# A retention layer and a gated feed-forward on one core: the same steps in another order, with other buffer slots

## Chip, cores and metric

One core of a Trainium2 chip runs the whole program in one launch. The metric is device time in microseconds (us) of that core; three runs of the kernel before are at hand, and one profiled execution with its trace. Engines are named as in the profile: PE (TensorE; PEld is its weight load), DVE (VectorE), ACT (ScalarE), POOL (GpSimd), SP (the queue that issues the DMAs).

## What is computed

For 4 batches, 8 heads, 768 positions and head size 64 a retention (linear attention with decay) is computed, and on its output a feed-forward with a convolution of three taps as gate:

```python
for t in range(S):
    state = gamma[None, :, None, None] * state + np.einsum('bhd,bhe->bhde', k[:, :, t], v[:, :, t])
    y[:, :, t] = scale * np.einsum('bhd,bhde->bhe', q[:, :, t], state)
...
h = np.maximum(x @ w_in, 0.0)                 # 512 -> 1024
...
for k in range(K):
    conv_out += conv_w[k][None, None, :] * hp[:, k:k + S, :]
gate = 1.0 / (1.0 + np.exp(-conv_out))
return (h * gate @ w_out).astype(np.float32)  # 1024 -> 512
```

## The kernel before, in words

All data are fp32. The retention is computed in chunks of 64 positions: 24 chunks `n` (two pairs of batches, 12 chunks each), all eight heads of both batches of a pair at once. Two chunks make a unit `u` of 128 positions (12 units), and on units the feed-forward works. There is no loop in the program that sets the order: every step has a name, and the string `ORDER` lists all 1352 of them; the program emits each step's instructions as it comes by in that list. Each engine then runs its own instructions strictly in that order and waits by semaphores for what others make.

The steps of a chunk `n` on PE are multiplications 64x64 in fp32: `scores/n` (k times q, into `ps_s`), `mix/n` (the masked scores times v into `ps_y`, together with the scores of the next chunk) and `across/n` (q times the state so far into the same `ps_y`, together with the new chunk's part of the state, into `ps_st`). A `mix` or an `across` has 32 such multiplications in two streams (16 at the first and last chunks of a pair), and each multiplication stands in the trace as two matmuls with two weight loads. Between them `masked/n` (DVE) multiplies the scores by the mask, `scale_v/n` scales v (on ACT or DVE), `carry/n` (ACT) copies the state from `ps_st` for the next chunk, and `decay/n` (DVE) reads `ps_y` and writes x.

Matrix products of the feed-forward are made in fp32r from split operands: a value is its rounded head and the rest, and three products (head x head, head x rest, rest x head) are summed. `x_head`, `x_rest` split x; the steps `w_...` split the weights, piece by piece as `load_w/i` brings them (0 to 7 of w_in, 8 to 15 of w_out, 16 the taps). `mm1/u/f` (12 matmuls 128x256 into `ps_m`) makes one block of 128 of the 1024 hidden features of a unit; `relu/u/p` (ACT) takes two such blocks to a buffer `h`; `seam` (POOL) copies or clears the border columns of `h` between units; `conv_tap` (ACT) and `conv_side` (DVE) compute the three taps; `gate` (ACT), `gated` (DVE), `g_head` (ACT) and `g_rest` (DVE) make the split factor `g`; `mm2/u/t/p/h` (6 matmuls 128x512, 256 columns at the very end) multiplies it by w_out into `ps_o`; `put` (ACT) and `store` (SP) bring it out. For units 8 to 11 the first product is made of seven smaller ones (`prod/v/j/q`, 12 matmuls each, a scheme with sums of operands: `sum_w`, `diff`, `head`, `sum_p`, `copy_p`), in place of `mm1`.

Buffers have numbered slots: `BUFS` says how many of a kind, and `SLOTS` gives, in order of use, which slot each new buffer takes (31 of `h`, 7 of `x`, 4 of `g`, 3 of `cv`, 2 of `ps_o`, `ps_y`, `ps_m`, `m` each). A step that writes a slot waits until the readers of its former content are done. `HELD` makes seven loads wait for a given step. Neither `BUFS` nor `HELD` differs in the new version.

Of the kernel before, what the change touches and what calls it, by code (L numbers as in the profile page):

```python
# [80 lines left out]
    w_shift/1 w_abs/2 mix/0 w_sign/1 w_clamp/2 w_shift/2 carry/0 load_kv/2 scores/1 w_power/1 load/3 w_head/1 load_w/3  # L81
    masked/1 load_w/16 scale_v/1 w_low/1 w_sign/2 mix/1 decay/0 across/1 make_gy/0 carry/1 w_head/2 w_rest/1 load_kv/3
    scores/2 load/4 decay/1 scale_v/2 masked/2 x_head/0 w_add/1 scores/3 x_head/1 w_power/2 w_abs/3 x_rest/0 mix/2
    x_rest/1 load_w/4 w_clamp/3 across/2 scale_v/3 w_shift/3 masked/3 mm1/0/0 load/5 w_low/2 load_w/5 w_rest/2 mm1/0/1
    w_sign/3 decay/2 w_head/3 w_add/2 carry/2 mix/3 w_abs/16 w_power/3 w_abs/4 w_rest/3 across/3 x_head/2 masked/4
    relu/0/0 w_low/3 mm1/0/2 load/6 scale_v/4 w_add/3 x_rest/2 mm1/0/3 carry/3 decay/3 w_clamp/4 x_head/3 w_shift/4
    mix/4 w_abs/5 x_rest/3 relu/0/1 w_clamp/5 across/4 make_gy/1 load_w/6 load_w/7 mm1/1/0 w_shift/5 w_sign/4 w_sign/5
    w_head/4 mm1/1/1 w_power/4 carry/4 w_power/5 w_head/5 masked/5 mm1/1/2 scale_v/5 w_rest/4 w_clamp/16 w_low/4
    relu/1/0 mm1/1/3 w_shift/16 load/7 scale_v/6 w_sign/16 w_add/4 w_power/16 w_low/5 mix/5 relu/1/1 decay/4 w_abs/6
    w_rest/5 across/5 w_clamp/6 w_low/16 w_add/5 mm1/1/4 carry/5 load/8 decay/5 load_w/8 x_head/4 masked/6 w_abs/7  # L90
    mm1/0/4 w_shift/6 w_add/16 w_sign/6 w_power/6 w_head/6 mix/6 make_gy/2 conv_tap/0/2 across/6 w_clamp/7 scale_v/7
    w_shift/7 masked/7 mm1/0/5 load/9 load_w/9 w_sign/7 carry/6 conv_tap/0/3 w_low/6 mm1/1/5 relu/0/2 w_rest/6
    w_head/7 seam/0/2/0 w_power/7 seam/0/1/0 w_add/6 mix/7 w_rest/7 w_abs/8 across/7 w_low/7 x_head/5 relu/1/2 w_add/7
    mm1/0/6 load/10 x_rest/4 w_clamp/8 x_rest/5 mm1/0/7 w_shift/8 scale_v/9 w_sign/8 mm1/2/0 relu/0/3 masked/8 w_abs/9
# [5 lines left out]
    seam/0/2/2 w_sign/11 mix/10 carry/9 load/12 conv_side/0/3/0 relu/2/1 conv_side/0/1/0 across/10 x_rest/6 scale_v/11  # L100
    masked/11 mm1/2/5 load/13 w_power/11 w_low/11 w_head/11 mm1/2/6 conv_side/0/2/2 carry/10 w_sign/10 relu/2/2
    w_power/10 w_head/10 mm1/3/0 conv_side/0/0/2 conv_tap/0/4 decay/10 scale_v/12 w_rest/11 mm1/3/1 decay/9 x_head/8
    conv_side/0/4/0 w_add/11 mm1/2/7 relu/3/0 w_low/10 load_w/14 x_head/9 w_rest/10 mix/11 relu/2/3 w_add/10 w_abs/12
    seam/2/3/0 across/11 load_w/15 seam/1/0/0 w_abs/13 masked/12 seam/1/1/0 w_clamp/12 seam/0/3/2 mix/12 x_rest/9
    load/14 seam/2/1/0 scale_v/13 seam/2/0/2 across/12 conv_side/0/1/2 w_shift/12 mm1/3/2 load/15 w_clamp/13
    w_shift/13 masked/13 mm1/3/3 w_sign/12 decay/12 x_rest/8 mm1/3/4 relu/3/1 w_sign/13 x_head/10 w_power/12 w_head/12
    mm1/3/5 w_low/12 gate/0/0 w_rest/12 conv_tap/0/5 carry/12 mm1/4/0 w_add/12 gated/0/0 w_abs/14 conv_side/0/5/0
    g_head/0/0 mm1/4/1 conv_side/0/4/2 relu/3/2 conv_side/0/3/2 decay/11 mix/13 g_rest/0/0 conv_side/0/5/2
    conv_tap/0/6 across/13 w_clamp/14 gate/0/1 w_power/13 masked/14 mm2/0/1/0/0 carry/13 load/16 scale_v/14
    conv_tap/0/7 x_rest/10 relu/4/0 mm1/3/6 x_head/11 gated/0/1 w_head/13 conv_side/0/6/0 w_rest/13 mm1/3/7  # L110
    conv_side/0/7/0 decay/13 mm2/0/0/0/0 w_low/13 conv_side/0/6/2 w_shift/14 mix/14 w_sign/14 g_head/0/1 relu/3/3
    g_rest/0/1 across/14 w_head/14 seam/3/3/0 conv_side/0/7/2 gate/0/2 seam/2/2/2 masked/15 mm2/0/0/1/0 load/17
    seam/1/1/2 conv_tap/1/0 gated/0/2 seam/3/1/0 carry/14 x_rest/11 gate/0/3 mm1/4/2 w_add/13 x_head/12 conv_tap/1/1
    scale_v/16 w_abs/15 mm1/4/3 w_power/14 x_head/13 conv_side/1/1/0 w_rest/14 g_head/0/2 w_clamp/15 mm2/0/1/1/0
    relu/4/1 w_low/14 seam/4/1/0 gated/0/3 seam/2/2/0 mm1/5/0 conv_side/1/0/0 seam/1/2/2 w_shift/15 seam/1/0/2
    g_rest/0/2 mm1/5/1 w_sign/15 conv_tap/1/4 scale_v/15 mm1/5/2 g_head/0/3 relu/5/0 g_rest/0/3 mm2/0/1/2/0
    conv_side/1/1/2 conv_tap/1/2 w_add/14 conv_tap/1/5 conv_side/1/0/2 mm1/5/3 decay/14 gate/1/0 x_rest/13 w_head/15
    mm1/4/4 conv_tap/1/3 conv_side/1/3/0 conv_side/1/2/0 mm2/0/0/2/0 w_power/15 conv_side/1/3/2 conv_side/1/2/2
    w_rest/15 mix/15 gated/1/0 across/15 g_head/1/0 masked/16 relu/5/1 conv_side/1/5/0 mix/16 load/18 g_rest/1/0
    seam/4/1/2 seam/1/3/2 w_low/15 conv_tap/1/6 mm1/5/4 seam/3/2/0 gate/1/1 seam/5/1/2 w_add/15 conv_side/1/5/2  # L120
    mm1/5/5 decay/15 conv_side/1/6/0 masked/17 mm1/4/5 gated/1/1 g_head/1/1 mm2/0/0/3/0 carry/15 g_rest/1/1
    conv_tap/1/7 relu/5/2 conv_side/1/7/0 across/16 conv_tap/2/0 conv_side/1/6/2 conv_side/1/4/0 scale_v/17
    conv_side/1/4/2 mm2/0/1/3/0 load/19 conv_side/1/7/2 gate/1/3 mm1/4/6 gate/1/2 put/0/1/0 gated/1/2 mm1/4/7
    g_head/1/2 put/0/0/0 g_rest/1/2 carry/16 gated/1/3 mm2/1/0/0/0 decay/16 g_head/1/3 conv_tap/2/2 g_rest/1/3 mix/17
    relu/4/3 conv_side/2/2/0 relu/4/2 conv_side/2/0/0 across/17 conv_tap/2/1 seam/4/2/2 x_head/14 seam/2/1/2
    mm2/1/0/1/0 load/20 conv_tap/2/4 seam/3/0/2 store/0/1/0 conv_tap/2/3 seam/4/3/0 conv_side/2/4/0 store/0/0/0
    seam/3/1/2 conv_tap/2/5 conv_side/2/1/0 seam/2/3/2 mm2/1/1/0/0 conv_side/2/2/2 seam/4/2/0 conv_side/2/3/0
    seam/4/0/2 conv_side/2/1/2 seam/5/0/0 conv_side/2/0/2 mm2/1/0/2/0 seam/3/3/2 conv_side/2/5/0 gate/2/0 seam/5/2/0
    masked/18 seam/3/0/0 x_head/15 conv_side/2/5/2 seam/4/0/0 mm1/5/6 carry/17 gated/2/0 seam/3/2/2 seam/5/1/0
    conv_side/2/4/2 g_head/2/0 seam/5/0/2 mm1/5/7 gate/2/2 g_rest/2/0 gated/2/2 mm2/1/0/3/0 conv_side/2/3/2 x_rest/15  # L130
    gate/2/1 gated/2/1 mm2/1/1/1/0 put/1/0/0 scale_v/18 relu/5/3 store/1/0/0 decay/17 seam/5/3/2 mm2/2/1/0/0
    g_head/2/1 conv_tap/2/6 conv_side/2/6/0 mix/18 scale_v/19 g_rest/2/1 across/18 masked/19 mm2/1/1/2/0 x_rest/14
    carry/18 load/21 conv_tap/3/0 decay/18 conv_tap/2/7 scale_v/20 x_head/16 mm2/1/1/3/0 conv_side/3/0/0 g_head/2/2
    conv_side/3/0/2 conv_tap/3/1 conv_side/2/7/0 mm1/7/0 conv_side/2/6/2 g_rest/2/2 x_rest/12 mm2/2/1/1/0
# [727 lines left out]
```

## Time and profile before

| | us |
|---|---|
| runs (three) | 335.62, 335.98, 338.96 |
| median | 335.98 |
| span of the profiled execution, first to last instruction | 335.6 |
| PE busy in it | 327.6 |
| DVE busy | 288.1 |
| ACT busy | 207.6 |

The span is one execution's time from its first to its last instruction; the runs' times are measured around whole executions without a profile. An engine's busy time counts overlapping instructions once. Matmuls are pipelined and their ends are modelled in the trace, so two matmuls that follow each other overlap.

### The profile page before, as it was taken

How to read it: one execution, taken by the hardware profiler on the slowest of the kernel's cores; microseconds unless marked ns; L12 is line 12 of the kernel's file. 1: busy time of each engine (PE TensorE's matmuls, PEld its weight loads, DVE VectorE, ACT ScalarE, POOL GpSimd, SP SyncE). 2: the span in 40 equal slices, each digit the busy share in tenths (PEclk: the TensorE clock that was granted, in tenths of full speed). 3: DMA queues.
4: the chain of work that ended last, by engine and by line, in shares of the span. 5: the costliest groups of instructions: out<-in, count | busy, mean ns of one | idle time of the engine just before them, and what ended most of it. 6: DMA issues, size and time to landing. Idle time of an engine off the chain costs nothing.

```text
span 335.6 us, 10804 instructions
## 1 busy us (share of the span) xinstructions
PE 327.6 (98%) x4666; PEld 293.4 (87%) x4666; DVE 288.1 (86%) x562; ACT 207.6 (62%) x430; POOL 24.2 (7%) x100
## 2 busy tenths in 40 slices
...
GB/s 248 350 366 323 229 296 281 273 273 241 182 127 128 2 128 127 191 93 158 100 33 26 166 2 34 32 0 34 31 2 31 34 0 64 2 63 0 64 63 63
DMA packets 10415, 40.77 MB, mean 121 GB/s; under 512 B 1280, under 2 KB 1792, under 8 KB 7808
## 3 DMA queue, kind: packets, MB, share of 16 engines
...
q8 instruction: 36, 0.59, 0.7%
...
## 4 chain that ended last, share of the span: by engine, by line
PE 96%; DVE 2%; issue 1%; ACT 0%; ACTq 0%; DVEq 0%
PE ps_o L783 40%; PE ps_m L570 27%; PE ps_s L390 6%; PE ps_m L690 5%; PE ps_y L690 5%; PE ps_st L390 5%; PE ps_y L390 4%; PE ps_o L312 3%; PE ps_s L690 2%; DVE rw L417 0%; DVE m L493 0%; DVE x L431 0%; DVE gy_sb L348 0%; DVE wi_lo L556 0%; DVE g L509 0%
## 5 line engine op out<-in xcount | busy, mean ns | idle before, releaser
L570 PE MATMUL ps_m<-xu,wi_hi 128*128 128x256 f32 x512 | 91.6, 281 | 0.0
L570 PEld LDWEIGHTS ps_m<-xu,wi_hi 128*128 128x128 f32 x512 | 78.9, 188 | 1.9
L570 PE MATMUL ps_m<-xu,wi_lo 128*128 128x256 f32 x256 | 71.5, 279 | 0.0
L783 PE MATMUL ps_o<-h,g 128*128 128x512 f32 (+1 forms) x200 | 63.4, 382 | 0.0
L390 PE MATMUL ps_y<-rw 64*64 64x64 f32 x1472 | 49.3, 220 | 1.7 <-issue 1.7
L570 PEld LDWEIGHTS ps_m<-xu,wi_lo 128*128 128x128 f32 x256 | 48.5, 189 | 0.0
L390 PEld LDWEIGHTS ps_y<-rw 64*64 64x64 f32 x1472 | 45.5, 135 | 2.4 <-issue 2.3
L754 ACT ACTIVATE cv<-cv 128x512 f32<-128x512 f32 x48 | 30.1, 629 | 21.9 <-DVE cv L748 21.9
L764 ACT CAST g<-cv 128x512 fp32r<-128x512 f32 x48 | 29.6, 618 | 21.9 <-DVE cv L759 17.3
L783 PEld LDWEIGHTS ps_o<-h,g 128*128 128x128 f32 x200 | 37.2, 188 | 6.7
L769 DVE TENSOR_TENSOR g<-cv,g 128x512 fp32r<-128x512 f32 x48 | 32.9, 689 | 10.5 <-ACT g L764 10.0
L748 DVE SCALAR_TENSOR_TENSOR cv<-h,cw_sb,cv 128x256 f32<-128x256 f32 x64 | 29.4, 479 | 1.4 <-ACT cv L743 1.2
L390 PEld LDWEIGHTS ps_s<-rw 64*64 64x64 f32 x768 | 24.7, 134 | 6.3 <-issue 3.4
L390 PE MATMUL ps_s<-rw 64*64 64x64 f32 x768 | 28.2, 221 | 1.3 <-DVE rw L417 1.0
L390 PE MATMUL ps_st<-rw 64*64 64x64 f32 x704 | 25.3, 219 | 0.9 <-ACT rw L358 0.6
L358 ACT ACTIVATE rw<-rw,consts_sb 128x128 f32<-128x128 f32 x64 | 20.4, 391 | 7.3 <-DMA rw<-in_qkv 7.3
L390 PEld LDWEIGHTS ps_st<-rw 64*64 64x64 f32 x704 | 22.8, 135 | 2.1 <-issue 0.8
L790 ACT COPY o_sb<-ps_o 128x512 f32<-128x512 f32 (+1 forms) x25 | 14.1, 565 | 12.1 <-PE ps_o L783 12.1
L417 DVE TENSOR_TENSOR rw<-ps_s,consts_sb 128x512 f32<-128x512 f32 x24 | 16.5, 686 | 4.4 <-PE ps_s L390 4.4
L743 ACT ACTIVATE cv<-h,cw_sb 128x256 f32<-128x256 f32 x32 | 16.0, 506 | 5.4 <-DVE g L769 5.4
L783 PE MATMUL ps_o<-h_g,g 128*128 128x512 f32 (+1 forms) x50 | 19.3, 388 | 0.0
L783 PE MATMUL ps_o<-h_m,g 128*128 128x512 f32 (+1 forms) x50 | 19.3, 388 | 0.0
...
## 6 DMA issues: line engine op xcount, KB each, us to landing
rw<-in_qkv SPq DMA_DIRECT2D x20, 1024.0 KB, 6.1
...
```

Of the source, the lines that this page charges most:

```text
L358: nc.scalar.activation(v[:, :, g], v[:, :, g], AF.Copy, scale=by[:, g : g + 1])
L390: nc.tensor.matmul(out, lhsT, rhs, start=start, stop=stop, skip_group_check=True)
L417: nc.vector.tensor_tensor(out=rw[n][:, 1], in0=s_ps.pop(n), in1=mask_sb.unsqueeze(1).broadcast_to([P, 2, NPAIR, C]), op=ALU.mult)
L570: nc.tensor.matmul(h_ps[u, p][:, odd], w[:, k, fs], x[:, k].rearrange("p b t -> p (b t)"), start=(i == 0), stop=(i == len(products) - 1),)
L690: nc.tensor.matmul(ps[:, i], w[k][:, fs], x[:, k].rearrange("p b t -> p (b t)"), start=(i == m == 0 and q in (1, 6, 5, 7)), stop=(m == len ...
L743: nc.scalar.activation(cvs[u, p][:, i], hs[u, p][:, i, :, 1 : P + 1], AF.Copy, scale=cw_sb[:, f, 1:2])
L748: nc.vector.scalar_tensor_tensor(out=cv, in0=h[:, :, k : k + P], scalar=cw_sb[:, f, k : k + 1], in1=cv, op0=ALU.mult, op1=ALU.add)
L754: nc.scalar.activation(cvs[u, p], cvs[u, p], AF.Sigmoid)
L764: nc.scalar.copy(gs[u, p][:, 0], cvs[u, p])
L769: nc.vector.tensor_tensor(out=lo, in0=cvs.pop((u, p)), in1=hi.bitcast(F32), op=ALU.subtract)
L783: nc.tensor.matmul(ps, g, w[f][:, cs], start=(f == 0 and i == 0), stop=(f == NF - 1 and i == 2))
L790: nc.scalar.copy(o[:, :n], o_ps.pop((u, t, h))[:, :n])
```

## The change

The list `ORDER` has the same 1352 steps. Its first 223 names are the same; from there on the steps stand in another succession, and the strings of `SLOTS` give the buffers other slots. On PE the two lists agree up to the end of `mix/9`, which lies between the first seven `mm1` steps of unit 1 and its last, `mm1/1/7`; behind it PE has `mm1/2/2` before and `across/9` now. A few functions are changed so that steps can stand in the new places: what was taken out of a dictionary at its last use now stays there, and a border column (`seam`) or a `relu` creates its buffer `h` if it is the first to touch it.

```diff
 SLOTS = {
-    "ps_o": "010101010101101001011001010",
-    "g": "0123012301230132001031203120312031203120312031203120312031203120",
+    "ps_o": "010110010101101001011010011",
+    "g": "0123012301230123012302130320130212302310231023120321032102302310",
...
-    "h": "0123456789abcdefghijklmnopqrstu0146235c9fdjilorpuc50639fjildoprujl9f",
-    "cv": "012102101201201201021020210212012012120012102012",
+    "h": "0123456789cabdfgijkelhomnqtprus0641253c9idflorj6up50c39dlifor5j6l0df",
+    "cv": "012102012201021020120120210121201021021002120102",
 }
 ORDER = """
...
-    w_low/8 w_sign/9 mix/8 decay/6 w_head/9 scale_v/10 across/8 masked/9 w_rest/8 mix/9 relu/2/0 load/11 w_power/9
...
+    across/8 masked/9 seam/1/2/0 sum_w/0/0 carry/8 w_rest/8 mix/9 across/9 load/11 seam/0/0/2 conv_side/0/0/2
...
     def masked(n):
-            out=rw[n][:, 1], in0=s_ps.pop(n), in1=mask_sb.unsqueeze(1).broadcast_to([P, 2, NPAIR, C]), op=ALU.mult
+            out=rw[n][:, 1], in0=s_ps[n], in1=mask_sb.unsqueeze(1).broadcast_to([P, 2, NPAIR, C]), op=ALU.mult
...
-        hs[u, p] = buf("h", [P, 2, 2, UH])
-        ps = h_ps.pop((u, p)).rearrange("p i (b t) -> p i b t", b=2)
-        nc.scalar.activation(hs[u, p][:, :, :, 1 : P + 1], ps, AF.Relu)
+        ps = h_ps[u, p].rearrange("p i (b t) -> p i b t", b=2)
+        nc.scalar.activation(inside(u, p), ps, AF.Relu)
...
-    def inside(u, p):
+    def h_of(u, p):
         if (u, p) not in hs:
             hs[u, p] = buf("h", [P, 2, 2, UH])
-        return hs[u, p][:, :, :, 1 : P + 1]
+        return hs[u, p]
+
+    def inside(u, p):
+        return h_of(u, p)[:, :, :, 1 : P + 1]
...
     def seam(u, p, side):
-        column = lambda v, i: hs[v, p][:, :, :, i : i + 1]
+        column = lambda v, i: h_of(v, p)[:, :, :, i : i + 1]
```

Place 1, PE at the end of `mix/9` (rows `ps_s` and `ps_y` with the chunks' buffers `rw`), before:

```order
L390 MATMUL ps_s_1218<-rw_1061 64x64 x2
L390 MATMUL ps_y_0_1217<-rw_946 64x64 x2
L570 MATMUL ps_m_0_1260<-xu_2_835,wi_hi_69 128x256 x2
L570 MATMUL ps_m_0_1260<-xu_2_835,wi_lo_70 128x256
L570 MATMUL ps_m_0_1260<-xu_2_835,wi_hi_69 128x256 x2
```

and now (`ps_st` is the state, which `across/9` adds to):

```order
L393 MATMUL ps_s_1223<-rw_1061 64x64 x2
L393 MATMUL ps_y_0_1222<-rw_946 64x64 x2
L393 MATMUL ps_st_193<-rw_946 64x64 x2
L393 MATMUL ps_y_0_1222<-rw_946 64x64 x2
L393 MATMUL ps_st_193<-rw_946 64x64 x2
```

`across/9` has moved up to `mix/9`, ahead of `mm1` steps of units 1 and 2.

Place 2, PE at the end of `across/17`, before:

```order
L390 MATMUL ps_st_1663<-rw_2011 64x64 x2
L390 MATMUL ps_y_0_2463<-rw_2011 64x64 x2
L783 MATMUL ps_o_0_2449<-h_g_1494,g_1_2348 128x512
L783 MATMUL ps_o_0_2449<-h_k_1593,g_1_2348 128x512
L783 MATMUL ps_o_0_2449<-h_g_1494,g_1_2348 128x512
```

and now:

```order
L393 MATMUL ps_st_1644<-rw_2300 64x64 x2
L393 MATMUL ps_y_0_2543<-rw_2300 64x64 x2
L393 MATMUL ps_s_2651<-rw_2648 64x64 x2
L393 MATMUL ps_y_1_2650<-rw_2330 64x64 x2
L393 MATMUL ps_s_2651<-rw_2648 64x64 x2
```

`mix/18` has moved up to `across/17`, where an `mm2` step stood; the same has been done with `mix/15` behind `across/14` and with `mix/21` behind `across/20`.

Place 3, SP's loads (`rw` of chunks 11 to 18, `g` of pieces 12 to 15 of w_out), before:

```order
L329 DMA rw_1253<-in_qkv 128x2048
L457 DMA g_0_1292<-in_w_out 128x1024
L457 DMA g_1_1335<-in_w_out 128x1024
L329 DMA rw_1413<-in_qkv 128x2048
L329 DMA rw_1469<-in_qkv 128x2048
L457 DMA g_3_1553<-in_w_out 128x1024
L457 DMA g_2_1614<-in_w_out 128x1024
L329 DMA rw_1658<-in_qkv 128x2048
L329 DMA rw_1695<-in_qkv 128x2048
L329 DMA rw_1875<-in_qkv 128x2048
L329 DMA rw_2011<-in_qkv 128x2048
```

and now:

```order
L332 DMA rw_1288<-in_qkv 128x2048
L460 DMA g_0_1507<-in_w_out 128x1024
L332 DMA rw_1576<-in_qkv 128x2048
L332 DMA rw_1630<-in_qkv 128x2048
L460 DMA g_3_1775<-in_w_out 128x1024
L332 DMA rw_1828<-in_qkv 128x2048
L332 DMA rw_1851<-in_qkv 128x2048
L460 DMA g_1_1926<-in_w_out 128x1024
L460 DMA g_2_1983<-in_w_out 128x1024
L332 DMA rw_2060<-in_qkv 128x2048
L332 DMA rw_2300<-in_qkv 128x2048
```

The last two pieces of w_out (`load_w/15`, `load_w/14`) have moved down behind `load/15`, directly ahead of `load/16`, and take slots of `g` that `mm2/0/0/0/0` and `mm2/0/1/1/0` read.

## Rows read from the trace of the kernel before

**Rows 1.** The page: span, then busy time, share and instructions of each engine.
```profile
span 335.6 us, 10804 instructions
...
PE 327.6 (98%) x4666; PEld 293.4 (87%) x4666; DVE 288.1 (86%) x562; ACT 207.6 (62%) x430; POOL 24.2 (7%) x100
```

**Rows 2.** Window: span, busy PE, PEld, DVE, ACT, POOL (count), PEclk, DMA share.
```profile
60.69:332.55 271.86, 270.54 (x3304) 244.03 (x3294) 235.91 (x462) 170.24 (x347) 22.04 (x86) 1.00 0.24 82
```

**Rows 3.** All waits of PE from 60 us on: total, times, longest.
```profile
PE ps_y L390 <- issue: 1.3, 1, 1.3
```

**Rows 4.** Timeline of PE around that wait: start, length, what.
```profile
80.42 0.28 PE L390 MATMUL ps_s<-rw 64*64 64x64 f32 x4
82.02 0.27 PE L390 MATMUL ps_y<-rw 64*64 64x64 f32 x2 [1.31 <-issue]
```

**Rows 5.** The page's DMA queues: packets, MB, share of 16 engines.
```profile
q8 instruction: 36, 0.59, 0.7%
```

**Rows 6.** Chain of work, in order of time: an earlier wait of PE.
```profile
27.09 0.30 issue
27.39 0.27 PE ps_s L390 x2
```

**Rows 7.** The same view, four stretches from 27.39 on.
```profile
27.39:60.56 33.17, 33.15 (x894) 32.04 (x897) 31.96 (x64) 21.72 (x50) 1.80 (x8) 1.00 0.79 275
27.39:69.67 42.28, 42.26 (x1149) 40.95 (x1152) 40.95 (x82) 26.94 (x60) 2.49 (x13) 1.00 0.77 270
27.39:78.08 50.69, 50.67 (x1277) 49.16 (x1280) 49.26 (x97) 32.44 (x74) 2.49 (x13) 1.00 0.78 270
27.39:82.02 54.63, 53.30 (x1403) 51.64 (x1403) 51.84 (x102) 35.33 (x79) 2.88 (x15) 1.00 0.78 268
```

**Rows 8.** DMA queue, five windows: 24.95:25.05, 79.7:79.8, 61:61.1, 73.05:73.15, 66.7:66.9.
```profile
q8 instruction: 1, 0.02, 55.2%
q8 instruction: 1, 0.02, 57.8%
q8 instruction: 1, 0.02, 75.3%
q8 instruction: 1, 0.02, 58.2%
q8 instruction: 1, 0.02, 38.9%
```

**Rows 9.** Chain of work: pieces in order of time (start, length, what).
```profile
58.81 0.20 PE ps_s L390 x2
...
61.85 5.85 PE ps_m L570 x48
67.70 0.20 PE ps_st L390 x2
...
98.23 1.36 PE ps_o L783 x6
99.59 0.20 PE ps_s L390 x2
101.61 1.59 PE ps_o L783 x6
103.20 2.83 PE ps_m L570 x24
```

**Rows 10.** Chain of work in windows 85:90 and 107.5:111.4: `mm1` alone.
```profile
84.99 5.10 PE ps_m L570 x45
107.43 4.01 PE ps_m L570 x34
```

**Rows 11.** The line of `masked`: duration in ns, shortest, median, longest.
```profile
L417 DVE TENSOR_TENSOR rw<-ps_s,consts_sb x24: 681/684/693, 10.6 to 195.2; 128x512 f32<-128x512 f32 x24
```

**Rows 12.** Two loads' issues (`load/16` at 93.94, `load/13` at 70.79): KB, us to landing.
```profile
rw<-in_qkv SPq DMA_DIRECT2D x1, 1024.0 KB, 5.3
rw<-in_qkv SPq DMA_DIRECT2D x1, 1024.0 KB, 8.1
```

More of the change, by code (lines that the diff above doesn't have):

```diff
@@ L80 @@
     w_shift/0 w_sign/0 w_abs/1 w_power/0 w_head/0 w_clamp/1 w_rest/0 scores/0 w_low/0 masked/0 scale_v/0 w_add/0
[L81 to L94, printed above, removed]
@@ L100 @@
[L100 to L114, printed above, removed]
@@ L115 @@
[L115 to L134, printed above, removed]
@@ L135 @@
-    conv_side/2/7/2 gate/2/3 mix/19 gated/2/3 across/19 g_head/2/3 conv_tap/3/2 g_rest/2/3 put/1/1/0 mm2/2/1/2/0
-    conv_tap/3/3 store/1/1/0 conv_tap/3/4 conv_side/3/3/0 load/22 x_head/17 mm1/6/0 conv_side/3/2/0 conv_tap/3/5
-    conv_side/3/4/0 conv_side/3/1/0 conv_side/3/1/2 mm2/2/0/0/0 gate/3/0 carry/19 gated/3/0 mm1/6/1 conv_side/3/3/2
-    conv_side/3/2/2 diff/0/0/3 mm2/2/0/1/0 scale_v/21 g_head/3/0 mm2/2/1/3/0 g_rest/3/0 decay/19 conv_tap/4/0
-    mm2/2/0/2/0 conv_side/3/5/0 conv_tap/4/1 diff/0/1/3 relu/6/0 masked/20 mm2/2/0/3/0 gate/3/1 conv_side/3/4/2
@@ L215 @@
-    conv_side/11/7/2 g_head/11/2 store/10/1/0 g_rest/11/1 gate/11/3 mm2/11/1/0/1 g_rest/11/2 mm2/11/0/1/0 gated/11/3
-    g_head/11/3 mm2/11/0/2/0 g_rest/11/3 mm2/11/0/3/0 mm2/11/1/1/1 put/11/0/0 mm2/11/1/2/1 store/11/0/0 mm2/11/1/0/0
-    mm2/11/1/1/0 mm2/11/1/2/0 mm2/11/1/3/0 mm2/11/1/3/1 put/11/1/0 store/11/1/0 put/11/1/1 store/11/1/1
+    w_shift/1 w_abs/2 mix/0 w_sign/1 w_clamp/2 w_shift/2 carry/0 load_kv/2 scores/1 w_power/1 load/3 w_head/1
+    load_w/3 masked/1 load_w/16 scale_v/1 w_low/1 w_sign/2 mix/1 decay/0 across/1 make_gy/0 carry/1 w_head/2
@@ new lines @@
+    w_rest/1 load_kv/3 scores/2 load/4 decay/1 scale_v/2 masked/2 x_head/0 w_add/1 scores/3 x_head/1 w_power/2
+    w_abs/3 x_rest/0 mix/2 x_rest/1 load_w/4 w_clamp/3 across/2 scale_v/3 w_shift/3 masked/3 mm1/0/0 load/5 w_low/2
+    load_w/5 w_rest/2 mm1/0/1 w_sign/3 decay/2 w_head/3 w_add/2 carry/2 mix/3 w_abs/16 w_power/3 w_abs/4 w_rest/3
+    across/3 x_head/2 masked/4 relu/0/0 w_low/3 mm1/0/2 load/6 scale_v/4 w_add/3 x_rest/2 mm1/0/3 carry/3 decay/3
+    w_clamp/4 x_head/3 w_shift/4 mix/4 w_abs/5 x_rest/3 relu/0/1 w_clamp/5 across/4 make_gy/1 load_w/6 load_w/7
@@ new lines @@
+    mm1/1/0 w_shift/5 w_sign/4 w_sign/5 w_head/4 mm1/1/1 w_power/4 carry/4 w_power/5 w_head/5 masked/5 mm1/1/2
+    scale_v/5 w_rest/4 w_clamp/16 w_low/4 relu/1/0 mm1/1/3 w_shift/16 load/7 scale_v/6 w_sign/16 w_add/4 w_power/16
+    w_low/5 mix/5 relu/1/1 decay/4 w_abs/6 w_rest/5 across/5 w_clamp/6 w_low/16 w_add/5 mm1/1/4 carry/5 load/8
+    decay/5 load_w/8 x_head/4 masked/6 w_abs/7 mm1/0/4 w_shift/6 w_add/16 w_sign/6 w_power/6 w_head/6 mix/6
+    make_gy/2 conv_tap/0/2 across/6 w_clamp/7 scale_v/7 w_shift/7 masked/7 mm1/0/5 load/9 load_w/9 w_sign/7 carry/6
@@ new lines @@
+    conv_tap/0/3 w_low/6 mm1/1/5 relu/0/2 w_rest/6 w_head/7 seam/0/2/0 w_power/7 seam/0/1/0 w_add/6 mix/7 w_rest/7
+    w_abs/8 across/7 w_low/7 x_head/5 relu/1/2 w_add/7 mm1/0/6 load/10 x_rest/4 w_clamp/8 x_rest/5 mm1/0/7 w_shift/8
+    scale_v/9 w_sign/8 mm1/2/0 relu/0/3 masked/8 w_abs/9 scale_v/8 carry/7 mm1/2/1 w_power/8 w_head/8 load_w/10
+    w_clamp/9 conv_tap/0/0 load_w/11 decay/7 mm1/1/6 w_shift/9 w_low/8 w_sign/9 mix/8 decay/6 w_head/9 scale_v/10
+    across/8 masked/9 seam/1/2/0 sum_w/0/0 carry/8 w_rest/8 mix/9 across/9 load/11 seam/0/0/2 conv_side/0/0/2
@@ new lines @@
+    seam/3/1/0 gated/0/0 seam/0/2/2 conv_side/0/4/2 conv_side/0/5/2 load_w/12 decay/8 x_head/8 seam/2/0/0 seam/0/3/0
+    w_power/10 masked/11 x_rest/8 scale_v/11 mm1/3/0 mm1/3/1 conv_side/0/3/2 mm1/3/2 mm1/3/3 carry/10 g_head/0/0
+    load/12 mix/11 across/11 conv_side/0/5/0 g_rest/0/0 load/13 decay/10 w_rest/10 w_low/10 w_add/10 w_head/11
+    scale_v/12 across/12 masked/12 mix/12 x_head/10 gate/0/2 gate/0/1 gated/0/1 decay/11 conv_tap/1/0 relu/3/0
+    x_head/9 x_rest/9 w_abs/12 w_clamp/12 g_head/0/1 relu/3/1 w_rest/11 w_add/11 mm1/3/4 mm1/3/5 w_shift/12 decay/12
@@ new lines @@
+    seam/3/3/0 seam/4/0/0 seam/1/1/2 mm2/0/1/0/0 scale_v/14 mm2/0/0/0/0 mm2/0/0/1/0 mm2/0/1/1/0 relu/4/1 scale_v/15
+    mix/13 load_w/15 w_abs/15 conv_side/0/6/0 across/13 carry/13 conv_side/0/7/2 conv_side/1/1/0 conv_side/1/1/2
+    masked/14 conv_tap/1/4 mm1/4/0 load_w/14 w_abs/14 w_clamp/14 gate/1/0 mm1/4/1 decay/13 relu/4/0 mm2/0/1/2/0
+    mm2/0/0/2/0 gated/1/0 gate/0/3 gated/0/3 w_shift/14 w_sign/14 w_head/14 mix/14 masked/15 g_head/0/3 load/16
+    seam/2/0/2 w_clamp/15 across/14 carry/14 w_shift/15 g_rest/0/3 g_head/1/0 mix/15 across/15 x_rest/11 mm1/5/2
@@ new lines @@
+    put/0/0/0 conv_side/1/3/2 load/18 conv_tap/1/7 conv_side/1/2/2 conv_side/1/7/0 x_head/12 seam/3/0/0 seam/4/2/0
+    seam/2/2/2 conv_side/2/0/0 gate/1/1 gated/1/1 conv_side/2/0/2 seam/2/1/0 conv_side/2/1/0 gate/2/0 gated/2/0
+    g_head/2/0 mm2/0/1/3/0 conv_side/1/7/2 g_rest/2/0 put/0/1/0 g_head/1/1 seam/4/3/0 mm2/1/1/0/0 mix/16 masked/17
+    conv_side/1/6/0 g_rest/1/1 across/16 decay/16 conv_tap/2/6 conv_tap/2/7 store/0/0/0 gate/1/3 mm1/5/4 mm1/5/5
+    store/0/1/0 mm2/1/0/0/0 x_head/14 conv_side/2/6/0 conv_tap/2/2 gated/1/3 relu/5/2 g_head/1/3 scale_v/18
@@ new lines @@
+    seam/3/2/0 mm2/1/0/1/0 mm2/1/1/1/0 mm2/1/1/2/0 g_rest/1/3 mm2/1/1/3/0 mm2/1/0/2/0 mm2/1/0/3/0 conv_side/2/7/2
+    conv_side/2/2/2 decay/15 conv_tap/2/3 conv_tap/2/4 conv_tap/2/5 conv_side/2/4/0 conv_side/2/4/2 carry/16
+    scale_v/17 mix/17 across/17 conv_side/2/3/2 conv_side/2/2/0 relu/5/0 conv_side/2/3/0 gate/2/1 gated/2/1
+    g_head/2/1 conv_side/2/5/2 g_rest/2/1 x_head/13 masked/18 carry/17 conv_tap/3/0 conv_tap/3/1 x_rest/12
+    conv_side/2/5/0 conv_side/2/6/2 put/1/0/0 conv_side/2/7/0 put/1/1/0 sum_w/1/1 gate/2/3 gated/2/3 gate/2/2
@@ new lines @@
+    conv_side/3/1/0 gated/2/2 g_head/2/3 g_rest/2/3 conv_tap/3/4 conv_tap/3/5 conv_side/3/0/0 conv_side/3/4/0
+    load/19 mix/18 conv_side/3/5/0 seam/5/2/0 seam/5/2/2 seam/3/2/2 masked/19 seam/3/0/2 conv_side/3/0/2 g_head/2/2
+    g_rest/2/2 across/18 carry/18 sum_w/1/2 mm1/5/6 mm1/5/7 relu/5/3 conv_tap/3/6 conv_side/3/6/2 conv_tap/3/7
+    x_rest/13 conv_side/3/1/2 gate/3/0 mm2/2/1/0/0 mm2/2/1/1/0 mm2/2/0/0/0 mm2/2/0/1/0 mm2/2/0/2/0 seam/6/3/0
+    seam/4/2/2 mm2/2/0/3/0 conv_side/3/5/2 conv_side/3/6/0 conv_side/3/4/2 gate/3/2 decay/18 decay/17 x_rest/14
@@ new lines @@
+    mm2/2/1/2/0 diff/0/0/3 mm2/2/1/3/0 x_head/16 scale_v/19 gated/3/0 g_head/3/0 g_rest/3/0 x_head/17 conv_tap/3/2
+    store/1/0/0 store/1/1/0 load/20 put/2/1/0 mix/19 across/19 put/2/0/0 seam/5/0/0 conv_tap/3/3 mm1/6/0 mm1/6/1
+    x_head/15 gated/3/2 g_head/3/2 diff/0/0/1 seam/4/1/2 conv_side/3/7/0 seam/5/1/0 x_rest/17 conv_side/3/2/0
+    conv_side/3/7/2 gate/3/3 relu/6/0 seam/3/1/2 seam/6/2/0 conv_side/3/2/2 diff/0/0/2 conv_side/3/3/2 scale_v/20
+    x_rest/15 conv_side/3/3/0 gated/3/3 g_head/3/3 g_rest/3/2 gate/3/1 gated/3/1 g_head/3/1 g_rest/3/1 decay/19
```

197 lines of the change are left out of this document (106 added, 91 removed).

## The prediction

> **What bounds the kernel now.** I began with the page's engine totals [rows 1]: the reader is to see that PE is busy for 327.6 of 335.6 us, DVE for 288.1, ACT for 207.6, POOL for 24.2. Then I cut the span at the place from which the two orders differ. PE's list is the same up to the end of `mix/9`, and from there to the last matmul the stretch is 271.86 us long with PE busy for 270.54 [rows 2]. The view of waits says what the missing 1.3 us are: from 60 us to the end PE waits once, and no semaphore releases it [rows 3]. The clock is full in that stretch (1.00 granted, the 2.4 GHz level) [rows 2]. So this is a kernel whose PE stream is gapless behind the change. DVE has 271.86 - 235.91 = 36 us to spare there, ACT 102 [rows 2]. A new order cannot win by relieving another engine; it can only change (a) that one wait, (b) what the PE stream itself costs by its succession, and (c) what it makes PE wait for anew.
>
> **The one wait is an instruction fetch.** PE stops inside `mix/12`, between multiplications that have no wait on them: four start from 80.42, the next from 82.02 [rows 4]. The reader is to see that the fetches of instructions are visible. There are 36 packets of 16 KB [rows 5], and PE's 4666 matmuls with as many weight loads [rows 1] are 9332 / 36 = 259 instructions to each packet, so near 256, a page. A second wait of that kind ends at 27.39 [rows 6]. Between 27.39 and 82.02 PE starts 1403 matmuls [rows 7], 2806 instructions, 10.96 times 256: both waits stand at a page's end. The fetch that the second one waited for starts between 79.70 and 79.80 and takes 0.578 x 16 x 0.1 us = 0.92 us [rows 8], so it ends near 80.7, and PE goes on 1.35 us later. For the wait that ends at 27.39 the fetch starts near 25.0 and takes 0.552 x 1.6 = 0.88 us [rows 8]: PE goes on 1.5 us after it. So a page can be used about 1.4 us after its packet.
> When is that late? A multiplication 64x64 in fp32 is two matmuls and two loads, so a `mix` or `across` of 32 of them is 128 instructions, half a page, and lasts about 1.0 us: two of them take 2.02 us (99.59 to 101.61), three 3.04 us (58.81 to 61.85) [rows 9]. A page of nothing else is gone in 2.05 us. A page with `mm1` or `mm2` steps lasts far longer (6 `mm2` matmuls alone 1.36 us [rows 9]).
> By the Trainium skill (Runtime: NRT & Kernel Launch, Instruction fetch mechanics) the sequencer fetches the next block of 256 instructions while it executes the current one, and the crossing is "mostly hidden". The trace agrees on the 256 and on most crossings, and differs in `mix/12`, where 1.3 us of idle time show. By that rule all waits below would be nothing, and the sum would fall by them; that is the first rival.
>
> **The change part by part.** Steps and their number are the same, so PE has the same matmuls.
> 1. *Whole pages of 64x64.* I counted 256 PE instructions to a page in the new list, from the page that starts at 60.56 (894 matmuls, 6.98 pages, after 27.39 [rows 7]). The old list behind `mix/9` has two whole pages of 64x64, one with a wait (`mix/12`) and one without. The new list has four: (a) `mix/9`, `across/9`; (b) from the last quarter of `mix/14` to the third quarter of `mix/15`; (c) from the end of `across/17` over `mix/18` to the end of `across/18`; (d) `across/20`, `mix/21`.
>  (a) can be priced: up to `mix/9` nothing differs, so its fetch is the old one, start 61.0 to 61.1, length 0.753 x 1.6 = 1.20 us [rows 8], end near 62.25, usable near 63.65. Before, `mm1/2/2` stood there and hid it. Now `across/9` starts when `mix/9` ends (61.8) and has 58 of its 64 matmuls in the old page, gone by 61.8 + 58/64 x 0.95 = 62.65. Wait: 1.0 us.
>  (b) to (d): the wait is lag of the fetch behind the page's start + its length 1.0 + 1.4 - 2.05. Lags of pages that start inside a 64x64 run: 0.5 (60.56 to 61.05) and 1.7 (78.08, 1277 matmuls after 27.39 [rows 7], to 79.75). That gives 0.85 and 2.05 us. The other end is zero: the run that begins at 67.70 [rows 9] has a whole page without a wait, since its fetch started at 66.7 to 66.9 [rows 8], before the run, with `mm1` ahead of it. I take 0.9 each, the smaller lag, because (b) to (d) lie where the loads are fewer than at 80 (DMA share over the whole stretch 0.24 [rows 2]). Sum of the four: 1.0 + 2.7 = **+3.7 us**, ends 1.0 and 7.2.
> 2. *The wait in `mix/12`* goes: its page now starts in `mm1/3/3`, with ten of its matmuls ahead of the run. From the start of one matmul to the next it cost 82.02 - 80.48 = **-1.5 us** (the four at 80.42 end at 80.70, one lasts 0.22).
> 3. *Fewer runs.* From `mix/9` on the old list has 14 separate runs of 64x64 steps, the new one 11: 17 and 18 are one run, 20 and 21 are one, and 14 | 15 with `mix/16` | `across/16` have become 14 with 15 | 16. (`across/9` only changes from one run to another.) The first `mm2` step behind a run takes 1.59 us, another 1.36 [rows 9]: 0.23 per run, 3 x 0.23 = **-0.7 us**; inside a run a step costs the same (2.02 / 2 and 3.04 / 3).
> 4. *Pace of `mm1`.* Two paces show: 45 matmuls in 5.10 us, 113 ns, and 34 in 4.01 us, 118 ns, the one from 84.99, the other from 107.43 [rows 10]. Behind an `mm2` step it is the slower one; behind a 64x64 run it is either. The old list has 18 `mm1` steps with no `mm2` between them and the run ahead, and 9 of them ran at 113; the new list has 52 such steps (`prod` among them). Half of 52 less 9 is 17 steps x 12 x 4.5 ns = **-0.9 us**, ends 0 and -2.3.
> 5. *The queues.* DVE: `masked/15`, `/18` and `/21` now stand between two blocks of one run, where only an `across` (0.95 us) covers them; one lasts 0.684 us [rows 11], and the same thing was hidden in the run at 58.81 [rows 9]. Behind each on DVE wait `decay` and the conv steps; cost 0, and 0.3 us each if DVE comes late. ACT: `carry/14`, `/17`, `/20`, single copies from `ps_st`, are covered by the next `mix`. SP: `load/16` is queued behind two `load_w` that now wait for `mm2` steps, and is issued when `across/13` ends. From there to `mix/15` PE has two `mm1` (2.83 us), two `mm2` (2.72 + 0.23) and `mix/14`, `across/14` (2.02), 7.8 us [rows 9]; loads took 5.3 and 8.1 us to land [rows 12], so 0, or 0.3. `load/13` likewise has about 8 us to `mix/12`. POOL's seams are 96 short copies beside 271 us; cost 0 while conv steps have DVE's 36 us behind them.
> 6. *The end* keeps its shape: 256-column `mm2` steps, a copy of ACT, a store. 0.
> Sum: 3.7 - 1.5 - 0.7 - 0.9 = +0.6 us. On the profiled span of 335.6 that is 336.2; the median of the runs (335.98) is 0.4 above that span, so I forecast **336.6 us**.
>
> **Rivals.** *First, the crossings are hidden* (the skill's rule): in (a) to (d) PE's sequencer runs ahead far enough, as it did at 66.8. Then -1.5 - 0.7 - 0.9 = -3.1 and the time is 332.9, with `mm1` at its best pace 331.5. For it: the run at 67.70. Against it: two waits at page ends, and (a), whose fetch is known.
> *Second, slower: a fetch falls behind a load.* The page that starts at 69.67 (1149 matmuls after 27.39 [rows 7]) had its successor's fetch only at 73.05 to 73.15 [rows 8], 3.4 us later, while loads of 1 MB were under way. A lag of 3.4 makes a wait of 3.4 + 1.0 + 1.4 - 2.05 = 3.75 us in place of 0.9. The place is (c): `load/20` waits for `across/17`, at whose end page (c) starts. If its packets come first there, +2.9: 339.5; at (d) with `load/23` too, 342.4. It decides itself by whether the fetch starts within about 1.5 us of the page's start. At 79.75 it came ahead of the load issued at about the same time, which speaks against it.
> *Third, a queue comes late in the doubled runs* (the 0.3 us of part 5, several times, or a conv chain): +1 to +3, 337.6 to 339.6.
>
> **How the numbers follow.** Forecast with waits at three or four of the places, 334.9 to 338.5: 0.62. Hidden crossings: 0.14, half of it beyond 1%. Fetch behind a load: 0.10. Late queues: 0.14, mostly within 1%. A measurement of this kernel cannot tell less than about 1% (3.4 us) from no change; the runs shown spread by that much. Faster by over 1%: 0.07; within: 0.80; slower: 0.13. The range leaves out the better half of the first rival and the far end of the second: 333.5 to 340.0.
>
> **What would show it.** Right: PE waits without a releaser at about 62.7 (1 us), in `mix/15`, `across/18` and `across/21`, none in `mix/12`; 36 fetches as before; PE otherwise gapless to the end, `mm1` stretches at 113 ns behind runs. Wrong: waits of PE with DVE or ACT as releaser, above all behind `masked` or `g_rest`; no waits in the four places; a gap of over 2 us at (c).

## The result

The new order is slower by 1.1%: 340.58 us is the median of its runs (338.45 to 344.05), 336.04 us that of the kernel before (333.64 to 341.3), the ratio 1.0113 with an interval of 1.0083 to 1.0143. The ratio leaves out runs that are over 1.5% above the fastest of their kernel, and so is not that of the two medians (1.0135). On 336.0 us that is +3.8 us (2.8 to 4.8), where +0.6 was forecast. The profiled execution has a span of 337.8 us, and the time of that run was 339.62: what lies around the span is 1.8 us, not the 0.4 that I read from a profile and a median of different runs. The profiled execution of before, with its span of 335.6, thus stood for a run of about 337.4, slower than the median run by 1.4.

The page of the new kernel (lines as in [rows 1] and [rows 5]):

```profile
span 337.8 us, 10784 instructions
...
PE 326.0 (96%) x4666; PEld 292.4 (87%) x4666; DVE 288.5 (85%) x562; ACT 207.5 (61%) x430; POOL 27.9 (8%) x100
...
q8 instruction: 36, 0.59, 0.7%
```

The waits of PE from 60 us to the end (total, times, longest), which answer to [rows 3]:

```profile
PE ps_y L393 <- issue: 2.3, 2, 1.2
PE ps_st L393 <- issue: 2.2, 2, 1.1
```

Four waits, none with a releaser, where before had one. The chain of work in four short windows shows where they stand (start, length, what; L573 is `mm1`):

```profile
62.78 1.11 issue
63.90 0.21 PE ps_st L393
...
109.78 1.14 issue
110.93 0.21 PE ps_y L393
...
146.46 1.05 issue
147.51 0.27 PE ps_st L393
147.85 0.32 PE ps_m L573
...
185.01 1.16 issue
186.17 0.27 PE ps_y L393 x2
```

By count of records they end in `across/9` (record 58), `mix/15` (47), `across/18` (58) and `across/21` (4): the ends of the pages (a) to (d) of the prediction, which had given the record for (a) and the place in the step for the others. From the start of one matmul to the next they take 1.33, 1.36, 1.27 and 1.38 us. The same window as in [rows 2], from the start of `mix/9` to the last matmul:

```profile
60.71:334.84 274.13, 269.66 (x3304) 243.40 (x3294) 236.44 (x462) 170.24 (x347) 24.82 (x88) 1.00 0.23 82
```

PE's 271.86 us have become 274.13, of which it is busy for 269.66: it has less to do by 0.9 us and stands still for 4.5. The fetches, read as in [rows 8] in four windows of 0.1 us (61.55, 108.4, 145.1 and 183.5 us on):

```profile
q8 instruction: 1, 0.02, 54.8%
q8 instruction: 1, 0.02, 66.9%
q8 instruction: 1, 0.02, 57.4%
q8 instruction: 1, 0.02, 75.4%
```

The first begins at 61.60 and lasts 0.548 x 1.6 = 0.88 us, the second begins at 108.45 and lasts 1.07, the third 0.92 from 145.17 on, the fourth 1.21 from 183.56 on; PE goes on 1.41 to 1.42 us after the end of each.

### The profile page after: what moved, and what is told of

Read it like the earlier page. It is cut to its first block, busy times and chain, and to the rows that moved or that the text cites. A ratio compares the mean times of both kernels' runs of the same rounds, so it can differ in the third digit from the quotient of the medians.

```text
span 337.8 us, 10784 instructions
## 1 busy us (share of the span) xinstructions
PE 326.0 (96%) x4666; PEld 292.4 (87%) x4666; DVE 288.5 (85%) x562; ACT 207.5 (61%) x430; POOL 27.9 (8%) x100
## 4 chain that ended last, share of the span: by engine, by line
PE 90%; DVE 3%; DMA 3%; issue 2%; SPq 1%; ACT 0%; DVEq 0%; ACTq 0%
PE ps_o L789 39%; PE ps_m L573 26%; PE ps_s L393 5%; PE ps_m L693 5%; PE ps_y L693 5%; PE ps_st L393 4%; PE ps_y L393 4%; DMA rw<-in_qkv 3%; PE ps_s L693 2%; DVE rw L420 1%; DVE x L434 1%; SPq L460 0%; DVE wi_lo L559 0%; DVE m L496 0%; DVE g L512 0%
## 5 line engine op out<-in xcount | busy, mean ns | idle before, releaser
L573 PE MATMUL ps_m<-xu,wi_hi 128*128 128x256 f32 x512 | 91.1, 282 | 0.0
L573 PEld LDWEIGHTS ps_m<-xu,wi_hi 128*128 128x128 f32 x512 | 77.6, 188 | 1.1
L573 PE MATMUL ps_m<-xu,wi_lo 128*128 128x256 f32 x256 | 71.3, 278 | 0.0
L789 PE MATMUL ps_o<-h,g 128*128 128x512 f32 (+1 forms) x200 | 62.5, 382 | 0.0
L573 PEld LDWEIGHTS ps_m<-xu,wi_lo 128*128 128x128 f32 x256 | 48.2, 188 | 0.0
L754 DVE SCALAR_TENSOR_TENSOR cv<-h,cw_sb,cv 128x256 f32<-128x256 f32 x80 | 36.7, 481 | 4.6 <-ACT cv L749 3.7
L393 PE MATMUL ps_st<-rw 64*64 64x64 f32 x704 | 26.0, 219 | 2.7 <-issue 2.2
L749 ACT ACTIVATE cv<-h,cw_sb 128x256 f32<-128x256 f32 x40 | 19.1, 504 | 1.6 <-DVE g L775 1.6
```

Of the source, the lines that this page charges most:

```text
L393: nc.tensor.matmul(out, lhsT, rhs, start=start, stop=stop, skip_group_check=True)
L573: nc.tensor.matmul(h_ps[u, p][:, odd], w[:, k, fs], x[:, k].rearrange("p b t -> p (b t)"), start=(i == 0), stop=(i == len(products) - 1),)
L749: nc.scalar.activation(cvs[u, p][:, i], hs[u, p][:, i, :, 1 : P + 1], AF.Copy, scale=cw_sb[:, f, 1:2])
L754: nc.vector.scalar_tensor_tensor(out=cv, in0=h[:, :, k : k + P], scalar=cw_sb[:, f, k : k + 1], in1=cv, op0=ALU.mult, op1=ALU.add)
L789: nc.tensor.matmul(ps, g, w[f][:, cs], start=(f == 0 and i == 0), stop=(f == NF - 1 and i == 2))
```

## The experiments

The theory under test, called the page theory: PE stands still where a page of 256 instructions holds nothing but 64x64 multiplications, since the next page's fetch is not there when the page is used up. (That the page must also begin deep in a run of them came out of the runs, most of all after_p64b.) Its rivals: the wait belongs to the long run and not to the page; or the time is lost elsewhere in the new order, in queues and slots. Ratios are against the kernel before in the same series of runs.

**before_again**: no edit.

> The kernel before, unchanged, as a control: ratio 1.000, interval about 0.003 to either side. The page theory (PE stands still where a page of 256 instructions holds nothing but 64x64 multiplications, since the fetch of the next page is not there when it is used up) expects the same wait in mix/12, 1.2 to 1.6 us, in a second profiled execution. If that wait comes and goes from execution to execution, it is absent here and the span falls by 1.5 us to about 334.0; then the typical time of before has no such wait, and that is why the measured difference (1.1%, some 3.8 us) is larger than that of the two profiled spans (2.2 us).

Ratio 1.0016 (0.9983 to 1.0049). This execution's span is 333.6 us, and PE has no wait at all behind 60 us. The window from the start of `mix/9` to the last matmul, with nothing idle in it:

```profile
60.23:330.55 270.32, 270.32 (x3304) 243.95 (x3294) 235.67 (x462) 170.16 (x346) 22.41 (x86) 1.00 0.23 83
```

So the wait in `mix/12` comes and goes. Its fetch, one row of the DMA queues in the window 76.7 to 76.8:

```profile
q8 instruction: 1, 0.02, 61.0%
```

Here it starts at 76.72, ahead of its page, which starts at 77.62; in the execution of [rows 8] it started at 79.75, 1.7 us behind the page's start at 78.08.

**after_split**: in each of the four long runs one step that stood beside it is moved in.

```diff
- mix/9 across/9 ... mm1/1/7
+ mix/9 mm1/1/7 across/9
- mm2/0/0/2/0 ... mix/14 ... across/14 ... mix/15
+ mix/14 ... across/14 mm2/0/0/2/0 ... mix/15
- mix/18 ... across/18 ... mm1/5/6
+ mix/18 ... mm1/5/6 across/18
- across/20 ... mix/21 ... across/21 ... mm1/6/7
+ across/20 ... mm1/6/7 mix/21 ... across/21
```

> The new order, but in each of the four long runs one mm1 or mm2 step that stood next to the run is moved into it (mm1/1/7 ahead of across/9, mm2/0/0/2/0 behind across/14, mm1/5/6 ahead of across/18, mm1/6/7 ahead of mix/21), so that no page holds only 64x64 multiplications; the number of instructions and every other step stay. Page theory: the four waits (1.05 to 1.16 us of idle time each, 5.3 us from start to start less 0.1) go, four more steps stand right behind a run (0.1 each): -4.8 us, span near 333.0, ratio to the kernel before 0.990 to 1.000. Rival, that the slowdown comes from other parts of the new order (late queues, slots) and the waits only stand where there is slack: the time stays, ratio 1.011. Rival, that a long run itself makes PE wait wherever its pages begin: the waits go as well here, so this run does not tell it apart from the page theory.

Ratio 1.001 (0.9977 to 1.0042), so 1.0% below the new order. PE has no wait behind 60 us, and the window from `mix/9` to the last matmul is 4.2 us shorter than that of the new kernel:

```profile
59.82:329.75 269.93, 269.84 (x3304) 243.04 (x3292) 235.98 (x462) 170.39 (x348) 26.83 (x88) 1.00 0.23 83
```

The other 1348 steps stand as in the new order. The whole loss was the four waits; its queues and slots cost nothing that shows.

**before_p48**: the order of before, its pages shifted.

```diff
-FILL = 6
+FILL = [128] * 12 + [256] * 6
...
```

The numbers are the columns of each filling multiplication at the start; the loop behind the dots takes them one by one.

> The kernel before with PE's instruction pages shifted by 48 instructions: the six filling multiplications of 512 columns at the start become 18 smaller ones with the same columns in all; nothing else differs. By count no page behind 30 us then holds only 64x64 multiplications. Page theory: the wait in mix/12 goes, -1.5 us, span near 334.0, ratio 0.994 to 0.998. Rival, that the wait belongs to the place in the run (mix/11, across/11, mix/12, across/12) and not to the page: it stays, ratio 1.000.

Ratio 1.0042 (1.0027 to 1.0056), span 334.3. No wait behind 60 us, and 270.2 us from `mix/9` (at 61.1) to the last matmul (331.3), as in before_again. The forecast of -1.5 us was against an execution with the wait; most have none, as the control showed, so the run says nothing of the wait's price. The start, whose pages are shifted too, was slower: `mix/9` stands at 61.1, against 60.2 there.

**before_p168**: the same with 48 fillings of 64 columns.

> The kernel before with its pages shifted by 168 instructions (48 filling multiplications of 64 columns in place of six of 512); its order of steps is that of before. By count four pages then hold only 64x64 multiplications, and they end inside mix/9 (record 38), across/10 (record 54), across/12 (record 24) and mix/16 (record 31). Page theory: waits of 1.0 to 1.4 us at these four places and none in mix/12, so 4 x 1.25 - 1.5 = +3.5 us, ratio near 1.010, as slow as the new order without any change of order. Rivals (the order of steps makes the time; or crossings of pages are hidden): ratio 1.000, no waits in these places.

Ratio 1.0761 (1.0717 to 1.0805), but not for the reason under test alone: the filling, which I took to be as long as before, lasts 20.7 us (8.4 before), as its line shows (busy, mean ns):

```profile
L313 PE MATMUL ps_o<-o_sb 128*128 128x64 f32 x96 | 20.7, 422 | 1.1 <-DVE o_sb L298 1.1
```

The waits stood where they were expected, in `mix/9`, `across/10`, `across/12` and `mix/16`, but the time could not be read, so the shift was made again with a short filling.

**before_p168b**:

```diff
-FILL = 6
+FILL = 4
+SHORT = 44
...
+        for i in range(SHORT):
+            nc.tensor.matmul(ps[:64, :64], warm[:64, :64], warm[:64, :64], start=True, stop=True)
```

> The shift of before_p168 (168 instructions) again, with a short filling: two of the six multiplications of 512 columns are left out and 44 multiplications 64x64 on zeros stand behind the others, so that the first chunk should start about when it did. Order of steps that of before. Page theory: waits of 1.1 to 1.8 us inside mix/9 (record 38), across/10 (54), across/12 (24) and mix/16 (31), and a smaller one in across/6 (record 60), whose page holds 124 of 128 matmuls of 64x64; together +5 to +7 us against an execution of before that has no wait in mix/12 (span 333.6): span 338.6 to 341, ratio 1.013 to 1.020. Rival, that the order of steps and not the pages makes the time: ratio 1.000, no waits there.

Ratio 1.0511 (1.0461 to 1.0561). The chain of work behind `mix/8`:

```profile
71.20 1.68 issue
72.89 0.21 PE ps_y L394
...
82.00 2.46 issue
84.45 0.27 PE ps_y L394
...
95.63 1.02 issue
96.65 0.45 PE ps_st L394 x7
...
133.47 1.10 issue
134.57 0.27 PE ps_y L394
```

The four waits end at the four records that the count gave, and the window from `mix/9` to the last matmul is 277.19 us, 6.9 longer than before_again's with the same order of steps:

```profile
70.40:347.59 277.19, 270.93 (x3304) 244.06 (x3295) 235.95 (x462) 169.88 (x346) 22.00 (x86) 1.00 0.23 81
```

The position of the pages alone thus costs more than the change did. The total was missed: `mix/9` starts at 70.4 us, 10.2 later than in before_again. The waits of PE without releaser in the first 58 us are:

```profile
PE ps_s L394 <- issue: 3.1, 2, 2.7
PE ps_y L394 <- issue: 2.0, 1, 2.0
...
PE ps_m L574 <- issue: 0.9, 1, 0.9
```

These are 6.0 us (against 1.6), all at ends of pages; the 2.0 is the smaller wait that was forecast in `across/6` at record 60, and it is the second longest of the start. The filling is longer, too: `scores/0` starts at 11.51 us and not at 8.66. And soon after each of the two longest waits the granted clock falls between its levels of 2.4 and 1.2 GHz: it is 0.60 in `across/2`, 0.71 in `mm1/0/5` and 0.56 in `mm1/1/5`, which take 6.5 us together, against 4.0 at 1.00 in before_again. 4.4, 2.85 and 2.6 us are 9.8 of the 10.2. For the price of the pages only the stretch from `mix/9` on is used.

**after_p64b**: the new order shifted by 64 instructions, with `FILL = 5` and 17 of the short multiplications.

> The new order with its pages shifted by 64 instructions (five filling multiplications of 512 columns in place of six, and 17 of 64x64). By count there are again four pages of nothing but 64x64, and they end 32 records earlier: inside across/9 (record 26, not 58), mix/15 (15, not 47), across/18 (26, not 58) and mix/21 (36 of 64, not across/21 record 4). Page theory: the four waits move there, 1.05 to 1.2 us of idle time each, the time stays that of the new order (ratio 1.008 to 1.014). Rival, that a run of four steps stalls by its own length: the waits stay at records 58, 47, 58 and 4.

Ratio 1.0228 (1.0176 to 1.0279), so above the forecast. The start is slow again: `mix/9` stands at 66.14, 5.4 us later than in the new kernel's first execution, and 4.4 of these are lost at the ends of two pages, in `mm1/0/3` and `across/4`. From `mix/9` to the last matmul it takes 273.8 us, against 274.1. The waits of PE from 58 us on:

```profile
PE ps_st L397 <- issue: 2.2, 3, 0.9
PE ps_o L793 <- ACT g L774: 1.1, 1, 1.1
PE ps_y L397 <- issue: 0.8, 1, 0.8
PE ps_m L577 <- issue: 0.2, 1, 0.2
```

Three of the four waits moved with the pages, to the records forecast in `across/9`, `across/18` and `mix/21`, and are gone from the old places, which refutes the run as their seat; at 0.7 to 0.9 us of idle time they are shorter than forecast. The fourth, in `mix/15`, did not come: its page now begins only 16 records into the run, and its fetch started 1.6 us ahead of the page. In its place two others stand. One is in `across/22` (0.7 us), whose page holds 121 of 127 records of 64x64. The other, of 1.1 us ahead of `mm2/4/0/0/0`, is put down to ACT's `g_head`, but it is a page's wait as well: `g_head` had ended 0.80 us before PE went on (where PE waits for a step of DVE or ACT elsewhere, it mostly goes on 0.05 us after it), while a page ends exactly there, and the packet of the next one had ended 1.37 us before. That fetch started at 193.81 us, 4.7 us behind the start of a page that holds `mm1` and `mm2` steps too, while loads and stores kept the DMA engines busy (share 1.00 from 190 to 192 us, 0.89 to 194). It is what the second rival of the prediction describes, seen at another place.

**before_a9**: one part of the change alone.

```diff
-across/8 masked/9 w_rest/8 mix/9 relu/2/0 ... carry/8 ... across/9
+across/8 masked/9 carry/8 w_rest/8 mix/9 across/9 relu/2/0 ...
```

> One part of the change alone: in the order of before, across/9 is moved up to the end of mix/9 (with carry/8, which it needs, ahead of mix/9); nothing else moves. Page theory: one wait of 1.1 us inside across/9 (record 58), 1.3 us from start to start, ratio 1.003 to 1.005, span 334.9 where no wait falls into mix/12. Rival, that the new order is slower by its queues or slots: ratio 1.000.

Ratio 1.0064 (1.0034 to 1.0095). One wait of a page, in `across/9` at record 58, 1.27 us from start to start, and one of 0.4 us in which `mix/12` waits for `masked/12` on DVE. PE's waits behind 60.6 us:

```profile
PE ps_st L390 <- issue: 1.0, 1, 1.0
PE ps_s L390 <- DVE rw L417: 0.4, 1, 0.4
```

A single moved step (with the `carry` that it needs) reproduces the first of the four waits, at its price. The ratio is 0.3% (0.9 us) above that price, which its interval still holds; the second wait, which the theory had not expected, is a part of that, and whether it comes with the move or by chance was not tried.

**after_again**: the new kernel, no edit.

> The new kernel unchanged, as a control on the same chip. Page theory: in a second profiled execution all four waits stand again at the same records (across/9 58, mix/15 47, across/18 58, across/21 4) with 1.0 to 1.3 us each, since their fetches are late by the pace of PE and not by chance; ratio 1.008 to 1.014. If some of the four are missing, the waits come and go as that in mix/12 does.

Ratio 1.0128 (1.0079 to 1.0177). All four waits again, at the same records; from start to start 1.23, 1.64, 1.06 and 1.29 us:

```profile
PE ps_y L393 <- issue: 2.5, 2, 1.4
PE ps_st L393 <- issue: 1.8, 2, 1.0
```

**before_split**: `mm1/3/2` moved from behind `across/12` to ahead of `mix/12`.

> The order of before with one step moved: mm1/3/2 from behind across/12 to ahead of mix/12, so that the one page that holds only 64x64 and sometimes makes PE wait (in mix/12, once in two profiled executions) is broken. Page theory, with a wait there in a part of the executions: its cluster of slower runs (336.2 to 337.4 us, against 335.2 to 335.9 for most) thins out, the median falls by 0 to 1.5 us, ratio 0.996 to 1.001; no wait of PE behind 60 us; from mix/9 to the last matmul 270.4 us, as in the execution of before without the wait. Rival, that these slower runs have another cause: median and spread as before, ratio 1.000.

Ratio 1.0022 (0.9987 to 1.0058), runs from 334.65 to 339.5: the spread did not shrink, so the slower runs of before are not mainly those with the wait. The window is 270.17 us, as in the executions without it. No gain that can be measured.

**before_look1, before_look2**: no edit.

> The kernel before, unchanged: a third profiled execution, for whether the wait in mix/12 is there. Page theory: either 0 or 1.2 to 1.6 us of wait there, and the stretch from mix/9 to the last matmul 270.3 or 271.9 us accordingly; nothing in between. Rival (the wait belongs to the order): 271.9 each time.

> The kernel before, unchanged: a fourth profiled execution, with the same two outcomes as the third.

Neither has the wait in `mix/12`; the two windows from `mix/9` on:

```profile
62.75:333.06 270.31, 270.31 (x3297) 243.95 (x3297) 234.99 (x460) 169.78 (x346) 23.18 (x86) 1.00 0.23 82
```

```profile
60.74:330.65 269.91, 269.91 (x3292) 243.52 (x3292) 235.63 (x462) 171.08 (x348) 22.70 (x86) 1.00 0.24 83
```

Spans of 336.1 and 333.7 differ by 2.4 us, 2.0 of which stand ahead of `mix/9` (62.75 against 60.74). A part of these is another wait that comes and goes. Before_look1 has it at 62.63 us, in `across/8`, 0.94 us from start to start:

```profile
PE ps_st L390 <- issue: 0.7, 1, 0.7
```

Its page holds five matmuls of `mm1/1/6` and then 123 of 64x64; the next page's fetch started 1.03 us behind the page's start there, and 1.0 to 1.8 us ahead of it in the other three executions of before. In these four executions the time ahead of `mix/9` varies by 2.5 us (60.23 to 62.75) and the stretch behind by 2.0 (269.9 to 271.9). The wait in `mix/12` stood in one of the four, the one that the prediction was worked out from.

## Why the prediction was right, and where it was wrong

The sign of the sum, the bound (a gapless PE stream) and the mechanism were right; the size was not: +0.6 forecast, +3.8 measured, and a loss of over 1% had been given a chance of 0.13. To compare the steps I summed PE's time from the start of each step to the start of the next, from `mix/9` on, by kind of step (us):

| | before, profiled | before_again | after | after_again | after_split |
|---|---|---|---|---|---|
| 64x64 steps (30) | 31.88 | 30.34 | 35.43 | 35.30 | 30.62 |
| `mm1`, `prod` (75) | 106.41 | 106.42 | 106.30 | 105.88 | 106.66 |
| `mm2` (100) | 133.56 | 133.57 | 132.41 | 132.38 | 132.66 |
| sum | 271.9 | 270.3 | 274.1 | 273.6 | 269.9 |

- *Part 1, whole pages.* Forecast +3.7, measured 35.43 - 30.34 = +5.1 (after_again 5.0). All four places were right. Page (a) was forecast at 1.0 and cost 1.33: its fetch started at 61.60 and not at 61.05 as in the execution before, and was shorter (0.88 for 1.20 us), so PE went on at 63.90 and not at 63.65; and the last matmul ahead of the wait started at 62.56, where 62.65 was taken. Pages (b) to (d) were taken at 0.9 with a lag of 0.5 us between the page's start and its fetch; the lags were 0.78, 0.91 and 0.72. The packets took 0.92 to 1.21 us (1.0 taken), the pages 1.90 to 1.99 from their first to their last matmul's start (2.05 taken), and PE went on 1.41 after a packet's end; this gives 1.25 to 1.39, near the 1.27 to 1.38 measured. The lag was the term most mis-sized, because I took the smaller of two that the trace showed.
- *Part 2, the wait in `mix/12`*, is the step that failed most. It was credited with -1.5 us as if each run of before had it. Three further executions do not have it: before takes 269.9 to 270.3 us there, not 271.9. Against the median run the change had nothing to remove. The 0.4 us by which I brought span and median together hid this: the right 1.8 would have shown that the profiled execution of before was slower than its median by 1.4.
- *Parts 3 and 4* were right in their sum: forecast -0.7 - 0.9 = -1.6, measured -1.3 (after_again -1.7). Part 3 had its size by luck. The 0.23 us for the first `mm2` step behind a run was read from pieces of the chain; from start to start it is 0.12 (1.50 against 1.37 us). But all ten such `mm2` steps are gone, and not three: -1.2 us. In their place seven more `mm1` steps stand right behind a run, each 0.09 us longer there: +0.6. Together that is -0.6, where -0.7 was forecast. Part 4 was right: the `mm1` and `prod` steps elsewhere went from 1.414 to 1.403 us, which is -0.7 over 64 of them, and to 1.397, -1.1, in after_again.
- *Part 5, the queues*, was right: PE waits for no other engine behind 61 us in either execution of the new kernel.
- With these sizes the sum is 5.1 - 0 - 1.3 = +3.8 us, which is what the runs show.

Of the rivals, the first (crossings are hidden) fell: at the four places they show, each time. The Trainium skill (Runtime: NRT & Kernel Launch, Instruction fetch mechanics) calls the crossing "mostly hidden"; 32 of the new kernel's 36 do cost less than 0.8 us here, but in whole pages of 64x64 it cost 1.0 to 2.7 us in 21 of the 31 profiled (the table at the end), so the measurement decides. The second (a fetch behind a load, +2.9) did not happen in the new kernel at (c) or (d), where the lags were the ordinary ones; the wait in `mix/12`, whose fetch came 2.6 us later than in before_again, may be of that kind, but what delayed it was not shown; in after_p64b a fetch did come 4.7 us late, with loads and stores under way. The third fell with part 5.
